# Output blocks of six groups: ScalarE copies and accumulating DMAs in place of VectorE sums, in a new order

## The chip, the core and the metric

The kernel runs on one core of a Trainium2 chip. Time is device time in microseconds (us) from launch to end; three runs of the kernel before are shown, and one further execution was profiled. TensorE multiplies matrices, VectorE and ScalarE work on elements, GpSimd and SyncE (SP) here only issue transfers, and 16 DMA engines move the data.

## The reference

For each of 8 batches an attention goes both ways between 512 tokens and 32 states of 8 heads, and a two-layer net follows on the 544 rows of each batch (4352 x 512 in all):

```python
a = softmax(scale * x @ state.T);   xread = a @ state        # [8, 8, 512, 64]
a2 = softmax(scale * state @ x.T);  sread = a2 @ x           # [8, 8, 32, 64]
r = concatenate([xread, sread], axis=2)                      # -> rows [8 * 544, 512]
h = r @ w_in                                                 # 512 -> 2048
g = where(h >= 1, h, where(h <= -1, 0, (h + 1) ** 2 / 4))
out = g @ w_out                                              # 2048 -> 512
```

## The kernel before

**Arithmetic.** Everything is float32, made of pairs of rounded float32 numbers: an operand is split into a high part (a ScalarE cast) and a low part (a VectorE subtraction), and each product is three matmuls, high by high, low by high and high by low. `xread @ w_in` is computed as `a @ (state @ w_in)`; the weight products `state @ w_in` of a batch are made in pieces (`sw_pair`), whose two parts are named sw_..h and sw_..l. The hidden rows of a batch come in eight units of 256 columns (`Hidden`: the matmuls at L718 to L720, then Relu and Square on ScalarE and a min/max, "bound", on VectorE at L744).

**The second layer.** Batch 0 multiplies by w_out directly (L779 to L781). The other seven are computed as blocks of 2 by 2 with seven products in place of eight: a group g takes a pair of batches and one half of the 2048 columns, so that the pairs (1, 2), (3, 4) and (5, 6) are groups 0 to 5; groups 6 and 7 ("wide", tiles of 384 columns) are batch 7 with the state rows of all batches. Each product k of 1 to 7 has four quarters (steps Qg.k.n, `quarter`, matmuls at L1329). Its operand is a block of hidden values or a difference of blocks, split again by ScalarE (L1292) and VectorE (L1266, `operand_ops`). Its weights are a block of w_out, or a sum of such blocks, of 1 MB, loaded from DRAM into one of eleven shared buffers (L1305, `weight_ops`; r and f are two names for such a buffer).

**Weight sums.** The blocks of w_out go to DRAM once they are split (L1234). For the sums, SP loads one half of a chunk (L1204), GpSimd adds the other half onto it by an accumulating DMA (also L1204), VectorE makes four sums (L1213 to L1216), ScalarE and VectorE split them (L1219, L1223), and SP stores the result (L1201, `block_ops`). There are eight chunks, D0 to D7; products 5, 6, 7 and 3 of a group need the sums of its four chunks.

**Outputs.** The products of a group run in three accumulators in PSUM. After each of the seven (`done_ops`) the accumulator is taken out: X after product 1, Y after 6, C22 after 7 and C21 after 4, all in one accumulator that goes on; V after 5 and C12 after 3; C11 after 2. The four output blocks of a pair are C11 + X, C12 + Y, C22 + V and C21, each summed over the pair's two groups. Before, they live in four buffers of 4 KB per partition ("one" 22, 23, 25, 26): in the first group of a pair ScalarE copies X, V, Y and C21 (L1368), and VectorE adds every other accumulator (L1366). After the second group SP stores the four blocks (L1382).

**Order.** The first 90 us (batch 0 and the splitting of the weights) stand in a table of their own, `ORDER`. The rest is planned when the program is built: `STEPS` sets the order of TensorE's steps (S weight products, X scores, R state reads, U units, G batch 0, Q quarters, L last units), and `Flow.schedule` places the steps of the other engines one by one where each could start first, by given costs and by `LATE`, the time from a step's end until another engine can use its result. On the chip each engine goes through its queue in that order, and waits for semaphores.

Of the kernel before, what the change touches and what calls it, by code (L numbers as in the profile page):

```python
# [13 lines left out]
ALU = mybir.AluOpType  # L14
# [138 lines left out]
class Flow:  # L153
# [4 lines left out]
    LATE = {"SP": 2.6, "PE": 0.3, "ACT": 0.12, "DVE": 0.12}  # L158
# [19 lines left out]
    def late(self, k):  # L178
        return self.LATE[self.ops[k][0]]

# [138 lines left out]
def state_exchange_moe(  # L319
# [17 lines left out]
    nc = tc.nc  # L337
# [695 lines left out]
    with guard:  # L1033
# [7 lines left out]
            r2_0={0: 0.0}, r2_1={0: 0.0}, xt={0: 0.0}, xn={0: 0.0}, z={0: 0.0}, e2={0: 0.0},  # L1041
        )
        flow.kinds.update({kd: (kd, len(flow.rooms[kd])) for kd in ("wc", "att", "tmp", "xt", "xn", "z", "e2", "r2_0", "r2_1")})
# [5 lines left out]
        flow.hold("spare", "spare", 8)  # L1049
        flow.rooms["pair"][10] = plan.done["g2", 1, 0, 6]  # L1050
# [17 lines left out]
        def load_ops(kind, b):  # L1068
            if kind == "xt":
                op(("dma", "xt", b), "SP", 2.6, lambda: load("xt", load_xt, b), take=[("xt", ("xt", b))])  # L1070
            else:
                op(("dma", "xn", b), "SP", 2.6, lambda: load("xn", load_xn, b), take=[("xn", ("xn", b))])
# [37 lines left out]
        def away_ops(b):  # L1110
            op(("away", b), "SP", 1.4, lambda: atts[b].trade_out(), [("exp2", b, 0), ("exp2", b, 1)],
               ends=[] if b == 1 else [("e2", b)])

        def read_ops(b):
            def m(name):
                return lambda: getattr(atts[b], name)()

            load_ops("xn", b)
            op(("trade", b), "SP", 1.4, m("trade_in"), [("away", b)], take=[("tmp", ("e2x", b))])
# [73 lines left out]
        def block_ops(c):  # L1193
# [31 lines left out]
            op(("wa", c), "SP", 1.4, lambda: whole(0), [("dA", c)], take=[("s", ("s", c))])  # L1225
            op(("wb", c), "SP", 1.4, lambda: whole(1), [("wa", c)])
# [3 lines left out]
            op(("dS", c), "SP", 2.6, lambda: store_block(1, place()), [("wsl", c)], ends=[("s", c)])  # L1230

        def keep_ops(c):
# [3 lines left out]
            op(("dA", c), "SP", 2.6, store, [("wol", c)] + ([] if c == NJ - 1 else [("g2", 1, 0, c)]), ends=[("wo", c)])  # L1236
# [4 lines left out]
        C_AT = {"X": 22, "V": 23, "Y": 25, "Z": 26}  # L1241
# [58 lines left out]
        def weight_ops(g, k):  # L1300
# [9 lines left out]
            op(h, "SP", 2.6, fetch_block, [("dA" if BLOCK[k] < 4 else "dS", 4 * (g % 2) + c) for c in range(4)],  # L1310
# [31 lines left out]

        def done_ops(g, k):
            odd = g % 2
            b0 = 1 + g // 2 * 2
            names = {1: ("X", "X"), 5: ("V", "V"), 6: ("Y", "Y"), 3: ("C12", "Y"), 7: ("C22", "V"), 2: ("C11", "X"), 4: ("C21", "Z")}
            name, where = names[k]
            c = ones[C_AT[where]].rearrange("p (d s) -> p d s", d=2)[:, :, :nn(g)]
            final = name[0] == "C"
            add = odd or name in ("C12", "C22", "C11")  # L1350
            need = [("q", g, k, 3)] + ([("away", 1)] if name == "Y" and not g else [])
            if final and k != 4:
                need.append(({"C12": "Y", "C22": "V", "C11": "X"}[name], g))
            if add and odd and not (final and k != 4):
                need.append(({"X": "C11", "V": "C22", "Y": "C12", "C21": "C21"}[name], g - 1))
            if not odd and not add and g:
                need.append(("go", {"X": "C11", "V": "C22", "Y": "C12", "C21": "C21"}[name], g - 1))
            ends = {3: [("B", g)], 2: [("C", g)], 4: [("A", g)]}.get(k, [])

            cut = [slice(d, d + 1) for d in range(2)] if g == 7 and final else [slice(0, 2)]  # L1360

            def evacuate():
                for d in cut:
                    src = chain(g, k)[:, d, :nn(g)]
                    if add:
                        nc.vector.tensor_tensor(out=c[:, d], in0=c[:, d], in1=src, op=ALU.add)  # L1366
                    else:
                        nc.scalar.copy(out=c[:, d], in_=src)  # L1368

            op((name, g), "DVE" if add else "ACT", nn(g) / 448 if add else nn(g) / 526, evacuate, need, ends=ends)  # L1370
            if final and odd:
                i, side = int(name[1]) - 1, int(name[2]) - 1

                def away():
                    if wide(g):
                        o = out[(B - 1) * S:].rearrange("r c -> (r c)")
                        o = o.rearrange("(i d p s t) -> i s p d t", i=2, d=2, p=P, s=2)[i, side]
                    else:
                        r0 = (b0 + side) * S + i * 2 * P
                        o = out[r0:r0 + 2 * P].rearrange("(d p) t -> p d t", p=P)  # L1380
                    for d in cut:
                        (nc.scalar if len(cut) == 2 and d.start else nc.sync).dma_start(out=o[:, d], in_=c[:, d])  # L1382

                op(("go", name, g), "SP", 1.4, away, [(name, g)])


        def sread_ops():
# [25 lines left out]
            op(("away", B), "SP", 1.4, away, [("scale2", b) for b in range(B)])  # L1413
            op(("trade", B), "SP", 1.4, back, [("away", B)], take=[("tmp", "sx")])
# [134 lines left out]
```

## Time and profile before

| | |
|---|---|
| runs shown, us | 616.03 median (615.67, 616.03, 618.26) |
| profiled execution, us | 619.75, of it the span from the first to the last instruction 618.0 |
| TensorE (PE) busy | 595.7 us (96%) |
| VectorE (DVE) busy | 521.4 us (84%) |
| ScalarE (ACT) busy | 402.3 us (65%) |
| GpSimd (POOL) busy | 7.8 us (1%) |
| moved by DMA | 136.97 MB |

Busy shares are of the span. Matmuls overlap: a row's duration is longer than the distance to the next start, and the distance is what a stream of matmuls costs. Queues of SP are shown as SPq; a DMA's landing time is from its issue to its last byte. Waits are attributed to what ended last before the waiting instruction began.

### The profile page before, as it was taken

Reading aid. Unit: us, or ns where it says so; the run is one execution under the profiler, and the core shown is the slowest. Engines: PE = TensorE matmul, PEld = TensorE weight load, DVE = VectorE, ACT = ScalarE, POOL = GpSimd, SP = SyncE. Lnnn points to the kernel's source line nnn. Section 1 sums busy time; section 2 is a strip of 40 time slices with the busy share of each in tenths; the row PEclk is TensorE's granted clock in tenths of the full one; section 3 lists DMA queues with packets and bytes.
Section 4 is the critical chain, followed back from the end, with each engine's and each line's share of the span. In section 5 each row is a group of like instructions: output and inputs, shape, how many; then the busy total and the mean of one; then the engine's idle time right before and its main releaser. Section 6 shows DMA issues by size and latency. Waiting matters only on the chain.

```text
span 618.0 us, 10299 instructions
## 1 busy us (share of the span) xinstructions
PE 595.7 (96%) x4208; PEld 481.3 (78%) x4208; DVE 521.4 (84%) x597; ACT 402.3 (65%) x512; POOL 7.8 (1%) x15
## 2 busy tenths in 40 slices
PE   5999988999999999999999999999999999999997
PEld 2677766677668877878777887788787888989996
DVE  6999977989799999799897987995769848785794
ACT  6999946966686556667656555765665456566741
POOL 0000100010100000000000000000000000000000
PEclk9999997999999999999999999999999999999999
DMA  8999999499976358655676148554727294434284
GB/s 357 425 370 374 362 351 353 153 262 308 291 231 218 98 159 303 187 205 171 203 275 197 43 142 284 167 193 137 230 78 272 86 313 158 139 125 137 79 281 151
DMA packets 81326, 136.97 MB, mean 222 GB/s; under 512 B 3200, under 2 KB 67328, under 8 KB 76160
## 3 DMA queue, kind: packets, MB, share of 16 engines
q1 hardware_dynamic: 79408, 131.28, 61.7%
q0 software_dynamic: 1152, 4.19, 3.7%
q10 hardware_dynamic: 720, 0.85, 0.4%
q8 instruction: 33, 0.54, 0.3%
q14 instruction: 13, 0.11, 0.1%
HBM read 105.91 MB, written 30.41 MB: 221 GB/s over the span
## 4 chain that ended last, share of the span: by engine, by line
PE 73%; DMA 12%; DVE 11%; issue 1%; ACT 1%; POOL 0%; POOLq 0%; DVEq 0%
PE bank L1329 39%; PE bank L718 8%; PE bank L720 8%; PE bank L719 8%; DMA f<-blocks 7%; PE bank L656 3%; DMA r<-blocks 3%; DVE r L1266 2%; DMA blocks<-f 2%; PE bank L779 1%; PE bank L620 1%; PE bank L780 1%; PE bank L781 1%; DVE one L1366 1%; DVE f L1223 1%
## 5 line engine op out<-in xcount | busy, mean ns | idle before, releaser
L1329 PE MATMUL bank<-r,r 128*128 128x512 f32 (+1 forms) x1344 | 301.1, 378 | 4.1 <-DVE r L1266 2.8
L1329 PEld LDWEIGHTS bank<-r,r 128*128 128x128 f32 x1344 | 245.7, 188 | 54.2 <-issue 8.9
L1292 ACT CAST r<-f 128x1024 fp32r<-128x1024 f32 (+1 forms) x140 | 113.1, 835 | 67.7 <-PE bank L1329 36.0
L1266 DVE TENSOR_TENSOR r<-f,r 128x1024 fp32r<-128x1024 f32 (+1 forms) x140 | 129.1, 950 | 10.6 <-ACT r L1292 10.4
L736 ACT ACTIVATE f<-bank,half 128x512 f32<-128x512 f32 x112 | 76.0, 687 | 63.9 <-PE bank L720 62.9
L744 DVE SCALAR_TENSOR_TENSOR f<-f,bank 128x1024 f32<-128x1024 f32 x56 | 67.7, 1211 | 26.8 <-ACT f L740 26.8
L740 ACT ACTIVATE f<-f 128x1024 f32<-128x1024 f32 x56 | 59.3, 1061 | 1.4
L1366 DVE TENSOR_TENSOR one<-one,bank 128x1024 f32<-128x1024 f32 (+2 forms) x44 | 46.3, 1058 | 9.7 <-PE bank L1329 8.1
L1266 DVE TENSOR_TENSOR f<-f,f 128x1024 f32<-128x1024 f32 x36 | 43.5, 1214 | 0.1
L656 PE MATMUL bank<-w,sb 64*32 64x256 f32 x1024 | 33.2, 381 | 2.9 <-DVE w L828 2.1
L1266 DVE TENSOR_TENSOR f<-f 128x384 f32<-128x384 f32 (+1 forms) x44 | 30.8, 732 | 0.1
L656 PEld LDWEIGHTS bank<-w,sb 64*32 64x32 f32 x1024 | 17.1, 106 | 14.0 <-issue 3.9
L779 PE MATMUL bank<-r,r 128*128 128x512 f32 x64 | 25.5, 399 | 0.0
L780 PE MATMUL bank<-r,r 128*128 128x512 f32 x64 | 24.9, 389 | 0.0
L781 PE MATMUL bank<-r,r 128*128 128x512 f32 x64 | 24.9, 389 | 0.0
L1368 ACT COPY one<-bank 128x1024 f32<-128x1024 f32 (+1 forms) x16 | 15.3, 958 | 13.0 <-PE bank L1329 10.7
L718 PE MATMUL bank<-ath,sw_0h 128*128 128x512 f32 (+1 forms) x56 | 21.3, 381 | 1.2 <-DVE one L744 0.8
L720 PE MATMUL bank<-atl,sw_0h 128*128 128x512 f32 (+1 forms) x56 | 21.0, 376 | 0.3 <-DVE atl L557 0.3
L719 PE MATMUL bank<-ath,sw_0l 128*128 128x512 f32 (+1 forms) x56 | 20.9, 374 | 0.0
L718 PE MATMUL bank<-ath,sw_2h 128*128 128x512 f32 x52 | 20.2, 389 | 0.0
L719 PE MATMUL bank<-ath,sw_2l 128*128 128x512 f32 x52 | 20.2, 389 | 0.0
L720 PE MATMUL bank<-atl,sw_2h 128*128 128x512 f32 x52 | 20.2, 389 | 0.0
(198 smaller groups left out, 898.6 us busy)
## 6 DMA issues: line engine op xcount, KB each, us to landing
r<-blocks SPq DMA_DIRECT2D x56, 1024.0 KB, 6.5
xt<-in_xt_dram SPq DMA_DIRECT2D x16, 512.0 KB, 7.4
f<-in_moe_w_in_dram SPq DMA_DIRECT2D x8, 1024.0 KB, 8.9
f<-in_moe_w_out_dram SPq DMA_DIRECT2D x8, 1024.0 KB, 11.2
blocks<-r SPq DMA_DIRECT2D x8, 1024.0 KB, 13.9
xn<-in_x_dram SPq DMA_DIRECT2D x8, 1024.0 KB, 6.3
blocks<-f SPq DMA_DIRECT2D x8, 1024.0 KB, 5.8
out_dram<-one SPq DMA_DIRECT2D x12, 512.0 KB, 7.2
```

Source lines behind the costliest of these rows:

```text
L656: nc.tensor.matmul(banks[hh][pr * NS:(pr + 1) * NS, cols], lhsT=sb[rows, b, pr], rhs=w32[c][rows, pr], start=True, stop=True,)
L718: nc.tensor.matmul(o, lhsT=wh[:, k, sl], rhs=ah[:, k, t], start=first, stop=False)
L719: nc.tensor.matmul(o, lhsT=wl[:, k, sl], rhs=ah[:, k, t], start=False, stop=False)
L720: nc.tensor.matmul(o, lhsT=wh[:, k, sl], rhs=al[:, k, t], start=False, stop=last)
L736: nc.scalar.activation(out=u, in_=h, func=AF.Relu, scale=0.5, bias=half)
L740: nc.scalar.activation(out=u, in_=u, func=AF.Square)
L744: nc.vector.scalar_tensor_tensor(out=u, in0=u, scalar=1.0, in1=h, op0=ALU.min, op1=ALU.max)
L779: nc.tensor.matmul(a, lhsT=lh, rhs=oh, start=f == 0, stop=False)
L1266: nc.vector.tensor_tensor(out=x, in0=y, in1=z, op=ALU.subtract)
L1292: nc.scalar.copy(out=o, in_=v)
L1329: nc.tensor.matmul(o, lhsT=lhs, rhs=v[:, e, a], start=fresh and n == m == 0, stop=n == 3 and m == 2, skip_group_check=not fresh,)
L1366: nc.vector.tensor_tensor(out=c[:, d], in0=c[:, d], in1=src, op=ALU.add)
```

## The change

In groups 0 to 5 ScalarE copies every accumulator (42 copies, 7 a group) into one of four rooms, "one" 22, 23, 25 and 26, which are now handed out by the planner. Each copy goes at once to its block in the output in DRAM: the first of a block by a plain store of SP, the others by a DMA of GpSimd that adds to what is there and waits until the block's transfer before has landed. A room is free again when its transfer has landed. Groups 6 and 7 keep the form of before (`last_ops`). The planner's times change: results of SP's transfers count as usable later (`LATE`, `MORE`), and `STEPS` is a new order of the same steps. Of that table two lines stand here.

```diff
 STEPS = (
-    "S1.1.1.2 X2 G0.7.0 U1.0 G0.7.1 U1.1 S2.0.2.1 U1.2 S1.3.1.4 U2.0 U1.3 U2.1 Q0.1.0 Q0.1.1 Q0.2.0 "
+    "S1.1.1.2 X2 G0.7.0 U1.0 U1.1 G0.7.1 S1.3.1.4 U1.2 S2.0.2.1 U1.3 Q0.2.0 U1.4 U2.0 Q0.1.0 Q0.2.1 "
...
-    LATE = {"SP": 2.6, "PE": 0.3, "ACT": 0.12, "DVE": 0.12}
+    LATE = {"SP": 3.6, "PE": 0.3, "ACT": 0.12, "DVE": 0.12}
+    MORE = {"wa": 2.4, "wb": 3.8, "dA": 5.0, "dS": 2.0, "away": 2.6, "trade": 1.4, "go": 1.5}
...
     def late(self, k):
-        return self.LATE[self.ops[k][0]]
+        return self.LATE[self.ops[k][0]] + self.MORE.get(k[0], 0.0)
...
+        NAMES = {1: "X", 5: "V", 6: "Y", 3: "C12", 7: "C22", 2: "C11", 4: "C21"}
+        BEFORE = {"C11": "X", "C12": "Y", "C22": "V"}
+        FINAL = {v: k for k, v in BEFORE.items()}
...
         def done_ops(g, k):
-            odd = g % 2
-            b0 = 1 + g // 2 * 2
...
-            add = odd or name in ("C12", "C22", "C11")
...
+            name = NAMES[k]
+            need = [("q", g, k, 3)]
             ends = {3: [("B", g)], 2: [("C", g)], 4: [("A", g)]}.get(k, [])
...
+            own = ("c", name, g)
+            block = FINAL.get(name, name)
+
+            def copy():
+                nc.scalar.copy(out=held(own, g), in_=chain(g, k))
+
+            def away():
+                if prior:
+                    nc.gpsimd.dma_start(out=out_of(g, name), in_=held(own, g), accum_op=ALU.add)
+                else:
+                    nc.sync.dma_start(out=out_of(g, name), in_=held(own, g))
+
+            prior = sent.get((g // 2, block))
+            sent[g // 2, block] = ("go", name, g)
+            op((name, g), "ACT", 0.97, copy, need, take=[("c", own)], ends=ends)
+            op(("go", name, g), "SP", 2.0 if prior else 1.45, away, [(name, g)] + [prior] * bool(prior), ends=[own])
...
             def evacuate():
                 for d in cut:
                     src = chain(g, k)[:, d, :nn(g)]
                     if add:
-                        nc.vector.tensor_tensor(out=c[:, d], in0=c[:, d], in1=src, op=ALU.add)
+                        nc.vector.tensor_tensor(out=c()[:, d], in0=c()[:, d], in1=src, op=ALU.add)
```

**VectorE's queue where the second layer begins.** f5 and f4 hold the first two weight chunks of the sums, nm2 and z2 belong to scores, sw1_1l is the low half of the weight product that TensorE's step U1.0 needs. Before:

```order
L1213 TENSOR_TENSOR f4_75<-f4_75 128x256
L1214 TENSOR_TENSOR f4_75<-f4_75 128x256
L1215 TENSOR_TENSOR f4_75<-f4_75 128x256
L1216 TENSOR_TENSOR f4_75<-f4_75 128x256
L1223 TENSOR_TENSOR f5_76<-f5_76 128x1024
L577 TENSOR_REDUCE nm2_0_801<-one24_96 128x1
L578 TENSOR_SCALAR nm2_0_801<-nm2_0_801 128x1
L501 STREAM_TRANSPOSE z2_805<-bank_69 128x1024
L672 TENSOR_TENSOR sw1_1l_760<-bank_69,sw1_1h_759 128x1024
L513 TENSOR_REDUCE m1_2_806<-z2_805 128x32
```

The same place now, where f9 is the second chunk:

```order
L1218 TENSOR_TENSOR f5_76<-f5_76 128x256
L578 TENSOR_REDUCE nm2_0_753<-one24_96 128x1
L579 TENSOR_SCALAR nm2_0_753<-nm2_0_753 128x1
L578 TENSOR_REDUCE nm2_0_753<-one24_96 128x1
L579 TENSOR_SCALAR nm2_0_753<-nm2_0_753 128x1
L1225 TENSOR_TENSOR f5_76<-f5_76 128x1024
L502 STREAM_TRANSPOSE z2_803<-bank_69 128x1024
L673 TENSOR_TENSOR sw1_1l_759<-bank_69,sw1_1h_758 128x1024
L514 TENSOR_REDUCE m1_2_804<-z2_803 128x32
L1215 TENSOR_TENSOR f9_80<-f9_80 128x256
L1216 TENSOR_TENSOR f9_80<-f9_80 128x256
```

The second chunk's sums moved from ahead of sw1_1l to behind it, and a second pair for nm2 moved ahead.

**An output of a second group.** On VectorE before, an accumulator (bank) is added to one22 among the bounds and splits of group 1's operands:

```order
L1266 TENSOR_TENSOR r8_90<-f10_81,r8_90 128x1024
L744 SCALAR_TENSOR_TENSOR f5_76<-f5_76,bank_69 128x1024 x2
L1366 TENSOR_TENSOR one22_94<-one22_94,bank_69 128x1024
L1266 TENSOR_TENSOR f5_76<-f5_76,f7_78 128x2x512
L1266 TENSOR_TENSOR r10_92<-f5_76,r10_92 128x1024
```

On ScalarE now, in group 1, two such accumulators are copied among its casts:

```order
L1293 CAST r0_82<-f10_81 128x1024
L1293 CAST r8_90<-f9_80 128x1024
L1370 COPY one26_98<-bank_69 128x1024
L737 ACTIVATE f7_78<-bank_69,half_104 128x512
L555 CAST ath4_1920<-zt4_1903 128x1024
L737 ACTIVATE f7_78<-bank_69,half_104 128x512
L741 ACTIVATE f7_78<-f7_78 128x1024
L1293 CAST r3_85<-f6_77 128x1024
L1293 CAST r2_84<-f9_80 128x1024
L1370 COPY one23_95<-bank_69 128x1024
```

The work went from VectorE's queue to ScalarE's, and the copy needs no earlier value of its buffer.

**GpSimd's queue.** Before, it ends with the eighth accumulation of weight chunks. Now outputs (out_0_dram) follow, 30 in all, the first of them between two chunks:

```order
L1206 DMA f2_73<-blocks_70 128x1024
L1374 DMA out_0_dram<-one23_95 128x2x512
L1206 DMA f7_78<-blocks_70 128x1024
L1206 DMA f2_73<-blocks_70 128x1024
L1374 DMA out_0_dram<-one22_94 128x2x512
L1374 DMA out_0_dram<-one23_95 128x2x512
L1374 DMA out_0_dram<-one25_97 128x2x512
```

The last two chunks' accumulations stand behind an output's.

## Rows read from the trace of the kernel before

**Rows 1.** The page's head and its busy times by engine.
```profile
span 618.0 us, 10299 instructions
...
PE 595.7 (96%) x4208; PEld 481.3 (78%) x4208; DVE 521.4 (84%) x597; ACT 402.3 (65%) x512; POOL 7.8 (1%) x15
```

**Rows 2.** Stretches: busy us (x instructions) by engine, granted clock, DMA share, GB/s.
```profile
30.00:90.00 60.00, 60.00 (x394) 45.62 (x392) 54.99 (x58) 49.06 (x51) 1.88 (x2) 1.00 1.00 363
90.00:110.00 20.00, 15.45 (x97) 11.59 (x104) 16.45 (x21) 13.49 (x20) 1.72 (x2) 0.83 1.02 364
110.00:180.00 70.00, 65.99 (x438) 48.35 (x418) 63.83 (x72) 53.33 (x69) 3.45 (x4) 1.00 0.81 242
180.00:500.00 320.00, 318.83 (x2419) 255.50 (x2419) 278.89 (x277) 195.49 (x233) 0.00 (x0) 1.00 0.57 186
...
590.00:618.00 28.00, 23.43 (x134) 22.82 (x132) 19.31 (x38) 7.28 (x15) 0.00 (x0) 1.00 0.63 205
```

**Rows 3.** Waits of TensorE: total us, times, longest.
```profile
PE bank L718 <- DVE sw_1l L672: 4.6, 1, 4.6
PE bank L1329 <- DVE r L1266: 2.8, 4, 1.2
...
PE bank L1329 <- DMA r<-blocks: 1.2, 2, 0.8
PE bank L718 <- DVE one L744: 0.8, 1, 0.8
PE bank L718 <- DVE one L1366: 0.8, 1, 0.8
```

**Rows 4.** TensorE in time: start, us, instruction, idle time before it.
```profile
89.73 0.39 PE L781 MATMUL bank<-r,r 128*128 128x512 f32 x1
94.67 0.80 PE L718 MATMUL bank<-ath,sw_7h 128*128 128x512 f32 x1 [4.55 <-DVE sw_1l L672]
...
99.96 0.52 PE L779 MATMUL bank<-r,r 128*128 128x512 f32 x1
100.31 0.39 PE L780 MATMUL bank<-r,r 128*128 128x512 f32 x1
```

**Rows 5.** VectorE in time, the same columns.
```profile
82.11 1.23 DVE L756 TENSOR_TENSOR r<-one,r 128x1024 fp32r<-128x1024 f32 x1
84.01 0.42 DVE L1213 TENSOR_TENSOR f<-f 128x256 f32<-128x256 f32 x1 [0.67 <-DMA f<-blocks]
...
88.88 0.42 DVE L1213 TENSOR_TENSOR f<-f 128x256 f32<-128x256 f32 x1 [3.31 <-DMA f<-blocks]
...
90.35 1.22 DVE L1223 TENSOR_TENSOR f<-f 128x1024 fp32r<-128x1024 f32 x1
...
92.27 1.24 DVE L501 STREAM_TRANSPOSE z<-bank 128x1024 f32<-128x1024 f32 x1
93.43 1.19 DVE L672 TENSOR_TENSOR sw_1l<-bank,sw_1h 128x1024 fp32r<-128x1024 f32 x1
```

**Rows 6.** The second accumulation: GpSimd in time; the chain of waits.
```profile
73.10 0.87 POOL L1204 DMA_DIRECT2D f<-blocks  x1 [0.18 <-issue]
...
73.10 15.75 DMA f<-blocks
```

**Rows 7.** The chain of waits: a run of matmuls without a pause.
```profile
363.53 9.52 PE bank L1329 x42
```

**Rows 8.** Groups of one form: busy us, mean ns, idle before.
```profile
L1366 DVE TENSOR_TENSOR one<-one,bank 128x1024 f32<-128x1024 f32 x30 | 36.3, 1214 | 1.1 <-PE bank L1329 0.7
...
L1368 ACT COPY one<-bank 128x1024 f32<-128x1024 f32 x12 | 12.1, 1010 | 10.1 <-PE bank L1329 7.8 <-PE bank L720 2.3
```

**Rows 9.** GpSimd's DMA queue; its issues; weight loads of 180 to 500 us.
```profile
q0 software_dynamic: 1152, 4.19, 3.7%
...
L1204 POOL DMA_DIRECT2D f<-blocks x8 | 7.1, 882 | 161.6 <-DVE z L536 70.6 <-DVE nm L578 24.9 <-DVE f L1266 24.8
...
DMA to landing us min/median/max: 5.4/6.1/11.4
```

More of the change, by code (lines that the diff above doesn't have):

```diff
@@ L1049, in state_exchange_moe @@
         flow.hold("spare", "spare", 8)
+        flow.hold("c", ("e2", 1), 25)
         flow.rooms["pair"][10] = plan.done["g2", 1, 0, 6]
@@ L1110, in away_ops @@
         def away_ops(b):
[L1111 to L1112 removed]
+            op(("away", b), "SP", 1.45, lambda: atts[b].trade_out(), [("exp2", b, 0), ("exp2", b, 1)],
+               ends=[("e2", b)])
         def read_ops(b):
@@ L1223, in sum_low @@
                 nc.vector.tensor_tensor(out=s.bitcast(F32R), in0=s, in1=place()[:, :1024], op=ALU.subtract)
-            op(("wa", c), "SP", 1.4, lambda: whole(0), [("dA", c)], take=[("s", ("s", c))])
-            op(("wb", c), "SP", 1.4, lambda: whole(1), [("wa", c)])
+            op(("wa", c), "SP", 1.45, lambda: whole(0), [("dA", c)], take=[("s", ("s", c))])
+            op(("wb", c), "SP", 1.45, lambda: whole(1), [("wa", c)])
             op(("ws", c), "DVE", 1.4, sums, [("wb", c)])
@@ L1229, in block_ops @@
             op(("wsl", c), "DVE", 1.14, sum_low, [("wsh", c)])
-            op(("dS", c), "SP", 2.6, lambda: store_block(1, place()), [("wsl", c)], ends=[("s", c)])
+            op(("dS", c), "SP", 2.75, lambda: store_block(1, place()), [("wsl", c)], ends=[("s", c)])
         def keep_ops(c):
@@ L1234, in store @@
                 nc.sync.dma_start(out=blocks[c // 4, 0, :, c % 4], in_=rounded(wo_at[c]).bitcast(F32))
-            op(("dA", c), "SP", 2.6, store, [("wol", c)] + ([] if c == NJ - 1 else [("g2", 1, 0, c)]), ends=[("wo", c)])
+            op(("dA", c), "SP", 2.75, store, [("wol", c)] + ([] if c == NJ - 1 else [("g2", 1, 0, c)]), ends=[("wo", c)])
         BLOCK = {1: 0, 2: 2, 3: 7, 4: 3, 5: 4, 6: 5, 7: 6}
@@ L1308, in fetch_block @@
                 )
-            op(h, "SP", 2.6, fetch_block, [("dA" if BLOCK[k] < 4 else "dS", 4 * (g % 2) + c) for c in range(4)],
+            op(h, "SP", 2.75, fetch_block, [("dA" if BLOCK[k] < 4 else "dS", 4 * (g % 2) + c) for c in range(4)],
                take=[("wt", h)])
@@ new lines, in state_exchange_moe, with out_of @@
+        BEFORE = {"C11": "X", "C12": "Y", "C22": "V"}
+        FINAL = {v: k for k, v in BEFORE.items()}
+        sent = {}
+        def out_of(g, name):
+            i, side = (int(v) - 1 for v in FINAL.get(name, name)[1:])
+            if wide(g):
+                o = out[(B - 1) * S:].rearrange("r c -> (r c)")
+                return o.rearrange("(i d p s t) -> i s p d t", i=2, d=2, p=P, s=2)[i, side]
+            r0 = (1 + g // 2 * 2 + side) * S + i * 2 * P
+            return out[r0:r0 + 2 * P].rearrange("(d p) t -> p d t", p=P)
@@ new lines, in held @@
+        def held(h, g):
+            return ones[flow.place[h]].rearrange("p (d s) -> p d s", d=2)[:, :, :nn(g)]
+        def done_ops(g, k):
+            name = NAMES[k]
+            need = [("q", g, k, 3)]
+            ends = {3: [("B", g)], 2: [("C", g)], 4: [("A", g)]}.get(k, [])
+            if wide(g):
+                return last_ops(g, k, need + [(b, g) for a, b in BEFORE.items() if a == name], ends)
+            own = ("c", name, g)
[11 more added lines that the diff above has]
+            op(("go", name, g), "SP", 2.0 if prior else 1.45, away, [(name, g)] + [prior] * bool(prior), ends=[own])
@@ L1362, in evacuate, with last_ops @@
+        def last_ops(g, k, need, ends):
+            odd, name = g % 2, NAMES[k]
+            block = FINAL.get(name, name)
+            own = ("c", block, B)
+            final = odd and name not in FINAL
+            c = lambda: held(own, g)
+            add = odd or name in BEFORE
+            if odd and name not in BEFORE:
+                need.append((block, g - 1))
+            cut = [slice(d, d + 1) for d in range(2)] if final else [slice(0, 2)]
             def evacuate():
@@ L1365, in evacuate @@
                     if add:
-                        nc.vector.tensor_tensor(out=c[:, d], in0=c[:, d], in1=src, op=ALU.add)
+                        nc.vector.tensor_tensor(out=c()[:, d], in0=c()[:, d], in1=src, op=ALU.add)
                     else:
[L1368 to L1372, printed above, removed]
+                        nc.scalar.copy(out=c()[:, d], in_=src)
+            op((name, g), "DVE" if add else "ACT", nn(g) / 448 if add else nn(g) / 526, evacuate, need,
+               take=[] if add else [("c", own)], ends=ends)
+            if final:
                 def away():
[L1375 to L1380, printed above, removed]
                     for d in cut:
-                        (nc.scalar if len(cut) == 2 and d.start else nc.sync).dma_start(out=o[:, d], in_=c[:, d])
-                op(("go", name, g), "SP", 1.4, away, [(name, g)])
+                        (nc.scalar if d.start else nc.sync).dma_start(out=out_of(g, name)[:, d], in_=c()[:, d])
+                op(("go", name, g), "SP", 1.45, away, [(name, g)], ends=[own])
         def sread_ops():
@@ L1411, in low @@
                 nc.vector.tensor_tensor(out=sl, in0=src, in1=sh.bitcast(F32), op=ALU.subtract)
-            op(("away", B), "SP", 1.4, away, [("scale2", b) for b in range(B)])
-            op(("trade", B), "SP", 1.4, back, [("away", B)], take=[("tmp", "sx")])
+            op(("away", B), "SP", 1.45, away, [("scale2", b) for b in range(B)])
+            op(("trade", B), "SP", 1.45, back, [("away", B)], take=[("tmp", "sx")])
             op(("kept", B), "DVE", 1.2, turn, [("trade", B)], ends=["sx"])
```

23 lines of the change are left out of this document (5 added, 18 removed), and 46 rows, old and new, of the table STEPS.

## The prediction

> **What bounds the kernel now.** I read the busy shares first: TensorE works through 595.7 of 618.0 us [rows 1], so a change can win at most what TensorE idles, plus what it loses to a low clock; a saving on another engine is worth nothing by itself. Next the stretches [rows 2], to see where those 22.3 us lie. From 90 to 110 us TensorE is busy for 15.45 of 20 us at a mean granted clock of 0.83. From 110 to 180 us it idles 4.01 us while VectorE is busy for 63.83 of 70. From 180 to 500 us it idles only 1.17 us, with VectorE at 87%, ScalarE at 61% and the DMA engines at 0.57. From 590 us on it idles 4.57 us, of which 1.2 is one wait [rows 3] and the rest the store behind the last matmul. What these leave of the 22.3, some 8 us, lies in the first 30 us, before the code that the change touches. Then the waits by name [rows 3]: the largest that the change can reach is 4.6 us, once, for the low half of a weight product (sw_1l); all others together are some 6 us in pieces of at most 1.2.
>
> That one wait is the place to look at closely. TensorE ends a matmul at about 90.1 us and starts the next at 94.67 [rows 4]. VectorE explains it [rows 5]: its queue is in order, and the four sums of the second weight chunk stood ahead of sw_1l. They waited 3.31 us for a transfer; then came the sums, their low half, a maximum, a transpose, and only then sw_1l. The transfer is an accumulating DMA of GpSimd, issued at 73.10 and 15.75 us in landing [rows 6]. And the idle time costs twice. Behind it matmuls start 0.43 us apart, at the lower of the two clock levels (1.2 GHz), until 99.96; the thirteen starts from 94.67 to 100.31 took 5.64 us [rows 4]. At the full clock a matmul of 512 columns takes 9.52/42 = 0.227 us [rows 7], thirteen 2.95. So the stall cost 4.55 + 2.69 = 7.2 us. The 4.01 us of short waits between 110 and 180 us left the mean clock there at 1.00 [rows 2].
>
> **Removed, added, moved.** *Output adds.* Thirty VectorE adds of 1.21 us go (36.3 us busy), and ScalarE copies of 1.01 us rise from 12 to 42, or 30.3 us more [rows 8]. Of this I count nothing: from 180 us on, where nearly all of it lies, TensorE has work in 99.6% of the time, and ScalarE goes from 61% to about 70% of that stretch. The cover is gone only where an engine queue runs late. The copy is shorter than the add that it replaces, so the matmuls that wait for a freed accumulator do not wait longer.
>
> *Transfers.* Twelve output stores of before become twelve plain stores and 30 accumulating ones. The trace has no accumulation into DRAM; nearest are GpSimd's eight accumulations from DRAM into SBUF, of the same 512 KB. Their queue took 3.7% of 16 engines' span [rows 9], 22.9 us for eight, so 2.9 us of all engines each. Bounds: a plain 512 KB transfer at half of this, and twice it for a read beside the write, so 1.4 to 5.8; I take 2.9, as the nearest row adds as well. Thirty make 86 us, which lifts the DMA share from 180 to 500 us from 0.57 to about 0.8. Who could wait? First the weight loads of TensorE (1 MB; 35 of them in that stretch landed in 5.4 to 11.4 us, median 6.1 [rows 9]). I counted in both orders the matmuls between the one that frees a load's room and the first that reads the load, at 0.227 us. In the order of before the room for a load is as short as 6.1 us and is under 10 us ten times; in the new order the shortest are 8.7 and 8.8 and the others 10.9 or more. A load that meets a whole accumulation lands after 6.1 + 2.9 = 9.0 us, which fits all but two. Second, ScalarE, whose copy waits until the transfer out of its room has landed, with all casts behind it. In the new order each of the four rooms is refilled no sooner than after 23.8 us of matmuls, and the longest landing of this kind of transfer was 15.75 us [rows 6]. So I take 1.2 us of TensorE idle time here, as before; the bounds are 0 and 6.
>
> The Trainium skill ("DMA: Bandwidth & Descriptors", section "Issuing engines are not separate DMA queues") says that transfers from SP, ScalarE and GpSimd run on the same 16 engines and interleave, whoever issues them; that speaks against the change. The trace agrees: the accumulation issued at 73.10, beside the loads and stores of 70 to 90 us, took 15.75 us [rows 6]. What this would make of the time is the third rival below.
>
> *New order at the stall.* In the new order VectorE's queue, from the same point (83.2 us, the end of the row at 82.11 [rows 5]), holds the sums of the first chunk alone, two maxima, their low half, the transpose, and sw_1l; the second chunk's sums stand behind it. By the durations of the same rows: sums from 84.01, if the first transfer lands as before, to 85.48; two maxima of 0.79 (90.35 to 92.27, less 1.13 for the low half) to 87.06; low half 88.2; transpose 1.16 to 89.35; sw_1l 1.19 to 90.5. TensorE reaches it at 90.1 as now, so 0.4 us of stall is left of 4.55, and a wait that short left the clock alone elsewhere. Gain: 4.15 + 2.69 = 6.8 us.
>
> *The stretch behind it.* TensorE now arrives some 7 us earlier, but VectorE does not work faster. I followed both queues to the third quarter of product 2 (Q0.2.2). VectorE has 33.3 us of work from 84.0 to that operand's low half (three chunks' sums at 1.47, sixteen operations and three low halves at 1.13, three transposes at 1.16, three maxima and some small ones): 117.3. TensorE has 102 matmuls at 0.227 and two weight products at 1.0 from 90.5: 115.7. So it stalls there for 1.6 us. The load for product 6 is issued when product 1 is done, and only 6.0 us of matmuls lie between; beside other transfers I expect 7.5 us, so 1.5 us (bounds 0 and 5). One more microsecond for what I did not follow makes 4.1 us, against the 4.01 of before. Gain here: 0; bounds 4 us better, 5 worse.
>
> *The end.* The last two groups keep their adds on VectorE and the last 27 us their kind of order; I leave its wait of 1.2 us as it is (bounds 0 and 2.5).
>
> **Sum.** 6.8 us less; of the profiled execution's own 619.75 us (span 618.0 and 1.75 around it) this makes 612.9. That execution is 3.7 us above the median of the runs shown, 616.03, and I carry the difference over: **609.2 us**. One measurement of this kernel tells about 0.5%, 3.1 us, from no change.
>
> **Rivals.** *More than the one stall goes.* The new order was drawn with longer transfer times, so other waits on late chunks may go too. If all of the idle time after 90 us goes (10.9 us, of it 4.55 the stall) with the 2.7 of the clock, 13.6 us are won: 602.4; half of the rest gives 605.8. For it speaks that every wait from 110 to 180 us is for VectorE [rows 3]; against it the 33.3 us of VectorE work just counted.
>
> *The stall moves.* VectorE was busy 63.83 of 70 us behind the stall [rows 2] and caught up while TensorE stood still. If 5 of the 6.8 us come back as waits for its operands before 180 us, the time is 614.2. Against it: its own idle time in the stretch, 3.31 us at one place [rows 5], goes as well.
>
> *Slower: accumulations delay the weight loads.* Place: matmuls of the first six groups, 180 to 500 us. If loads landed in 12 us instead of 6.1, the thirteen with under 12 us of matmuls in the new order would wait 14.0 us in sum: 616.0 - 6.8 + 14 = 623.2. It decides from about 11.3 us of landing, where the waits eat the 6.8. For it: the longest loads took 11.4. Against it: the median, and a DMA share of 0.8 on average.
>
> *GpSimd issues late.* The Trainium skill ("SBUF — State Buffer", the box on the trap in which VectorE blocks a GpSimd DMA) warns that GpSimd cannot write descriptors while VectorE holds their shared port. The eight issues of before took 0.88 us each [rows 9], all in stretches in which VectorE was busy over 80% of the time [rows 2], so the trace shows none of it. As a mechanism of this kernel: transfers issued late hold their rooms longer, and the copies, casts and matmuls wait. It takes over 8 us of delay on top of the longest landing before the first room is late; with ten copies held 1 us each it gives 619.
>
> **How the numbers follow.** Forecast 0.62, with its own range 605 to 613 (the first stall sure within 1 us, the stretch behind it from 4 better to 5 worse, the middle up to 5 worse); more goes 0.15; the stall moves 0.12; slower loads 0.08; late issues 0.03. Faster by over 0.5% (below 612.9): 0.60 + 0.15 = 0.75. Slower (above 619.1): the loads and part of the late issues, 0.09. Within: 0.16. The range 603.5 to 616.5 leaves out the best third of the first rival and all of the slow ones.
>
> **What would show it.** Right: no TensorE idle time over 1 us near 90 us, granted clock 1.00 from 90 to 110, VectorE's sw_1l ahead of the second chunk's sums; a wait of 1 to 3 us near 117; VectorE some 35 us less busy, ScalarE 30 more, both without effect; 180 to 500 us (now some 7 us earlier) still with TensorE over 99% busy. Wrong: weight loads with a median over 10 us and TensorE waits for them of several microseconds; ScalarE copies that wait for an output transfer; or a TensorE stall over 3 us elsewhere before 180 us with the clock down behind it.

## The result and the profile after

The changed kernel takes **623.17 us** (median of 18 executions, 616.25 to 627.11); the kernel before, on the same chip, took 615.73 (613.56 to 619.51). The ratio is 1.0092, 95% interval 1.0064 to 1.0119: **slower by 0.9%**, where 609.2 us and a gain were forecast. Ratios, here and below, compare executions in the faster state and are not quotients of the medians, which would give 1.012 here. The profiled execution is the longest of the 18, 627.11 us; run 12 below shows a shorter one.

The page, with GpSimd's DMA queue [rows 1, 9]:

```profile
span 625.3 us, 10392 instructions
...
PE 598.9 (96%) x4208; PEld 482.3 (77%) x4208; DVE 489.1 (78%) x567; ACT 429.0 (69%) x542; POOL 43.8 (7%) x45
...
q0 software_dynamic: 9312, 19.93, 19.0%
```

The waits of TensorE [rows 3]:

```profile
PE bank L1330 <- DMA r<-blocks: 14.8, 5, 6.5
...
PE bank L1330 <- DVE sw_0l L673: 0.8, 1, 0.8
...
PE bank L1330 <- ACT r L1293: 0.6, 1, 0.6
```

The span is 7.3 us longer. TensorE idles 26.4 us instead of 22.3, and is busy 3.2 us longer with the same 4208 matmuls; 2.0 of that is time at the low clock (4.7 us, worked out below, against 2.7). The weight product's 4.6 us wait is gone from the list; 14.8 us for weight loads stand at its head, where 1.2 stood. VectorE is 32 us less busy and ScalarE 27 us more, and neither ends a long wait. The stretches [rows 2], in the same columns, and three short ones around two waits:

```profile
90.00:110.00 20.00, 19.22 (x138) 14.31 (x137) 19.55 (x23) 17.69 (x23) 1.72 (x2) 1.00 1.04 357
110.00:180.00 70.00, 63.91 (x433) 47.82 (x431) 58.69 (x68) 49.86 (x66) 5.94 (x6) 0.98 0.90 272
180.00:500.00 320.00, 310.17 (x2334) 246.72 (x2335) 244.32 (x244) 211.28 (x250) 28.66 (x24) 0.98 0.82 223
...
147.00:153.00 6.00, 5.99 (x78) 4.59 (x79) 2.40 (x3) 0.66 (x3) 0.00 (x0) 0.72 0.28 89
170.00:186.00 16.00, 9.45 (x55) 6.97 (x53) 13.23 (x14) 9.94 (x12) 3.01 (x3) 0.87 1.05 287
186.00:192.00 6.00, 6.00 (x70) 3.26 (x70) 0.14 (x1) 1.01 (x1) 0.00 (x0) 0.50 0.22 62
```

From 90 to 110 us the loss is gone: 3.77 us more of TensorE's work, at a clock of 1.00 instead of 0.83. VectorE in time shows how [rows 5]:

```profile
87.40 1.24 DVE L502 STREAM_TRANSPOSE z<-bank 128x1024 f32<-128x1024 f32 x1
88.57 1.18 DVE L673 TENSOR_TENSOR sw_1l<-bank,sw_1h 128x1024 fp32r<-128x1024 f32 x1
...
90.80 0.41 DVE L1215 TENSOR_TENSOR f<-f 128x256 f32<-128x256 f32 x1
```

The low half stands ahead of the second chunk's sums and is done at 89.75, just before TensorE begins U1.0 at 89.84; and those sums no longer wait either (no idle time stands on the row). U1.0 does not read this low half: its operands are sw_7h and sw_7l [rows 4], pieces of a weight product made earlier. By the kernel, what it waited for before is a pair of PSUM banks to write into, free once the low half, the last operation to read them, is done. In run 13 below U1.0 runs ahead of that low half.

What was lost lies behind. TensorE in time, at the first quarters of products 6 (Q0.6) and 4 (Q0.4) of group 0:

```profile
147.01 2.31 PE L1330 MATMUL bank<-r,r 128*128 128x512 f32 x6 [4.30 <-DMA r<-blocks]
...
185.89 2.93 PE L1330 MATMUL bank<-r,r 128*128 128x512 f32 x6 [6.55 <-DMA r<-blocks]
188.75 3.57 PE L657 MATMUL bank<-w,sb 64*32 64x256 f32 x64
```

Both wait for their weights. The chain of waits gives the loads' issue and time to landing, 10.82 and 15.47 us:

```profile
136.05 10.82 DMA r<-blocks
...
170.38 15.47 DMA r<-blocks
```

After each the clock is down: 0.72 from 147 to 153 us and 0.50 from 186 to 192, so 6.0 x 0.28 + 6.0 x 0.50 = 4.7 us more. The two waits cost 10.85 + 4.7 = 15.5 us, twice what the 90 us stall cost. Behind 190 us there are three more, of 0.25, 1.94 and 1.75 us. All but the wait at Q0.4 are known at this size from this one execution only. The DMA engines while the load for product 4 (Q0.4) is under way, 170 to 186 us (queues; issues with KB and median us to landing):

```profile
q1 hardware_dynamic: 1870, 3.00, 53.4%
q0 software_dynamic: 560, 1.57, 51.6%
...
f<-blocks POOLq DMA_DIRECT2D x2, 512.0 KB, 9.9
r<-blocks SPq DMA_DIRECT2D x1, 1024.0 KB, 15.5
e_there<-one SPq DMA_DIRECT2D x1, 512.0 KB, 16.1
out_dram<-one POOLq DMA_DIRECT2D x1, 512.0 KB, 13.6
e_x<-e_there SPq DMA_DIRECT2D x4, 128.0 KB, 14.8
```

Nine transfers, the load among them, the first six issued within two us: the 16 engines are full until it lands (share 1.05). One of the nine is an accumulation into the output; two are accumulations for the weight sums of group 1, issued at 170.16 and 171.37; in the kernel before these two came at 156.71 and 169.12. By the Trainium skill ("DMA: Bandwidth & Descriptors", section "Issuing engines are not separate DMA queues") transfers run on the same 16 engines and interleave, whichever engine starts them; the trace agrees: SP's queue (q1) and GpSimd's (q0) share the engines, and their shares sum to the full.

The copies and the accumulations as groups [rows 8]:

```profile
L1370 ACT COPY one<-bank 128x1024 f32<-128x1024 f32 x42 | 42.5, 1013 | 34.5 <-PE bank L1330 34.3
L1374 POOL DMA_DIRECT2D out_dram<-one x30 | 36.2, 1208 | 335.5 <-ACT one L1370 319.9 <-issue 8.1 <-DMA out_dram<-one 7.5
```

Landing of the accumulations, of the weight loads of 110 to 180 us, and of those of 180 to 500 us [rows 9]:

```profile
DMA to landing us min/median/max: 5.4/9.1/13.6
...
DMA to landing us min/median/max: 7.4/10.0/15.5
...
DMA to landing us min/median/max: 5.4/8.3/13.9
```

q0's 19.0% of 625.3 us is 118.8; the eight accumulations of the weight sums keep 22.2 (first run below), so 96.6 for 30, **3.2 us of all 16 engines each**, where 2.9 was forecast. ScalarE's copies wait for TensorE alone, never for a transfer out of their room.

### The profile page after: what moved, and what is told of

Read it like the earlier page. It is cut to its first block, busy times and chain, and to the rows that moved or that the text cites. A ratio compares the mean times of both kernels' runs of the same rounds, so it can differ in the third digit from the quotient of the medians.

```text
span 625.3 us, 10392 instructions
## 1 busy us (share of the span) xinstructions
PE 598.9 (96%) x4208; PEld 482.3 (77%) x4208; DVE 489.1 (78%) x567; ACT 429.0 (69%) x542; POOL 43.8 (7%) x45
## 3 DMA queue, kind: packets, MB, share of 16 engines
q0 software_dynamic: 9312, 19.93, 19.0%
## 4 chain that ended last, share of the span: by engine, by line
PE 84%; DMA 12%; DVE 2%; ACT 1%; issue 1%; SPq 0%; ACTq 0%
PE bank L1330 42%; DMA r<-blocks 10%; PE bank L719 9%; PE bank L721 9%; PE bank L720 9%; PE bank L657 5%; PE bank L780 2%; PE bank L781 2%; PE bank L782 2%; DMA out_dram<-f 1%; PE bank L621 1%; PE bank L485 1%; DMA sb<-in_state_dram 1%; ACT f L737 0%; ACT r L1293 0%
## 5 line engine op out<-in xcount | busy, mean ns | idle before, releaser
L1330 PE MATMUL bank<-r,r 128*128 128x512 f32 (+1 forms) x1344 | 302.2, 380 | 16.7 <-DMA r<-blocks 14.8
L1370 ACT COPY one<-bank 128x1024 f32<-128x1024 f32 x42 | 42.5, 1013 | 34.5 <-PE bank L1330 34.3
L1374 POOL DMA_DIRECT2D out_dram<-one x30 | 36.2, 1208 | 335.5 <-ACT one L1370 319.9
L657 PE MATMUL bank<-w,sb 64*32 64x256 f32 x1024 | 35.0, 395 | 0.5 <-DVE w L829 0.5
```

Source lines behind the costliest of these rows:

```text
L657: nc.tensor.matmul(banks[hh][pr * NS:(pr + 1) * NS, cols], lhsT=sb[rows, b, pr], rhs=w32[c][rows, pr], start=True, stop=True,)
L1330: nc.tensor.matmul(o, lhsT=lhs, rhs=v[:, e, a], start=fresh and n == m == 0, stop=n == 3 and m == 2, skip_group_check=not fresh,)
L1370: nc.scalar.copy(out=held(own, g), in_=chain(g, k))
```

## Experiments

Theory A: the accumulations delay the weight loads. Theory B: the new order bunches transfers, so that loads come late even without them. The "30 left out" below are the accumulating output transfers; those accumulators then never reach the output. Medians are in us, ratios against the kernel before on the same chip.

| run | median | ratio, 95% interval |
|---|---|---|
| changed kernel | 623.17 | 1.0092 (1.0064 to 1.0119) |
| 1 the 30 left out | 614.37 | 0.9978 (0.9955 to 1.0001) |
| 2 the 30 as plain stores | 617.96 | 1.0025 (1.0000 to 1.0049) |
| 3 old steps, new outputs | 655.99 | 1.0639 (1.0597 to 1.0681) |
| 4 new steps and times, old outputs | 638.15 | 1.0373 (1.0329 to 1.0416) |
| 5 Q0.4 later | 614.14 | 0.9956 (0.9922 to 0.9990) |
| 6 Q0.4 and Q0.6 later | 624.34 | 1.0112 (1.0086 to 1.0138) |
| 7 group 0's three left out | 617.07 | 1.0012 (0.9983 to 1.0042) |
| 8 both later, the 30 left out | 623.20 | 1.0088 (1.0059 to 1.0117) |
| 9 Q0.4 later, the 30 left out | 610.49 | 0.9897 (0.9870 to 0.9925) |
| 10 Q0.4 later, Q0.6 by a quarter | 649.75 | 1.0547 (1.0500 to 1.0594) |
| 11 X3 later | 634.07 | one execution |
| 12 changed kernel again | 625.34 | 1.0154 (1.0088 to 1.0220) |
| 13 old steps and outputs, new times | 630.47 | 1.0206 (1.0164 to 1.0249) |
| 14 new steps and outputs, old times | 630.52 | 1.0214 (1.0167 to 1.0261) |

**1 and 2. The transfers.**

```diff
-                    nc.gpsimd.dma_start(out=out_of(g, name), in_=held(own, g), accum_op=ALU.add)
+                    return                                                   # run 1
+                    nc.gpsimd.dma_start(out=out_of(g, name), in_=held(own, g))   # run 2
```

> The changed kernel without its 30 accumulating output transfers (so 30 of the 42 copied accumulators never reach the output); every other instruction stands where it stood. Theory A, the accumulations delay the weight loads: the loads' median landing goes back from 8.0 to about 6.1 to 6.5 us, the waits of 4.3 us (Q0.6) and 6.6 us (Q0.4) shrink to under 2 us each, the TensorE clock behind them stays at 1.00, and the time is 605 to 611 us. Theory B, the new order bunches the loads itself (at 170 us a weight load, a trade, two chunk accumulations stand within 2 us, and only one output transfer): at least 8 of the 10.9 us at these two places stay, and the time is 614 to 620 us.

> The changed kernel with the 30 accumulating transfers turned into plain stores to the same place from the same queue (the sums are left out, the last accumulator written stands in the output). Every instruction stands where it stood. If what hurts is the work that an accumulation is for the DMA engines (about 3.2 us of all 16 each, by the queue's 118.8 us less some 23 for the eight chunk accumulations), half of it goes: loads land in about 7 us and the time is 612 to 618 us, between the run without the transfers and the changed kernel. If what hurts is the queue or the moment of issue and not the volume, the time stays at 619 to 625 us. If only the new order hurts, it is within 3 us of the run without the transfers.

Run 1, the waits of TensorE:

```profile
PE bank L1330 <- DMA r<-blocks: 6.6, 3, 5.5
```

The load for Q0.4 in its chain of waits:

```profile
167.14 14.41 DMA r<-blocks
```

And its stretch from 180 us:

```profile
180.00:500.00 320.00, 318.41 (x2381) 255.37 (x2382) 245.80 (x247) 217.18 (x257) 0.00 (x0) 0.99 0.56 184
```

Their q0, of run 1:

```profile
q0 software_dynamic: 1152, 4.19, 3.6%
```

and of run 2:

```profile
q0 software_dynamic: 5472, 19.93, 9.9%
```

Both theories hold a part. Without the transfers the wait at Q0.6 is gone (its load lands in 6.67 us instead of 10.82; run 12 shows that it can be gone with them too), loads from 180 to 500 us land in 6.0 us (median) and make no wait there apart from Q0.4's, and 1.1% is won back, less than theory A claimed. But Q0.4 still waits 5.49 us, for a load that takes 14.41: that wait belongs to the order. A plain store costs (61.0 - 22.2) / 30 = 1.3 us of all engines, an accumulation 2.5 times as much, and run 2 lies between run 1 and the changed kernel: what hurts is the engines' work, and not GpSimd's queue alone, which has the same 30 transfers in run 2.

**3 and 4. The order and the outputs apart.** Run 3 is the changed kernel with the `STEPS` of before, run 4 the kernel before with the new `STEPS`, `LATE` and `MORE`.

> The changed kernel's outputs (42 copies, 12 plain stores, 30 accumulating transfers) with the order of steps of the kernel before. Theory A: the 90 us stall of 4.6 us with its low clock is back, and room for a weight load is as short as 6.1 us and under 10 us ten times in this order, so waits for loads sum to 15 us or more from 110 us on: 625 to 640 us. Theory B: the loads of the old order are not bunched, the stall is back, and the time is that of the kernel before, 613 to 620 us.

> The kernel before, outputs summed on VectorE, with the new order of steps and the new late times of the planner. Theory A: the gain of 6.8 us at 90 us stays and little is given back, 605 to 611 us, with Q0.6 and Q0.4 waiting under 2 us each. Theory B: long waits for the weight loads of Q0.6 and Q0.4 (4 us and more) stand here too, 614 to 620 us. A third way, VectorE's 30 adds that stand between its other work in an order drawn without them: waits of TensorE for VectorE's operands of 5 us and more from 110 to 180 us, 614 to 622 us.

TensorE's waits in run 3, and in run 4:

```profile
PE bank L1330 <- DMA r<-blocks: 29.2, 10, 7.3
```

```profile
PE bank L719 <- DVE sw_2l L673: 5.1, 1, 5.1
...
PE bank L657 <- DVE f L745: 3.7, 1, 3.7
PE bank L657 <- DVE sw_6l L673: 3.3, 1, 3.3
```

Run 3 is worse than theory A asked: in the old order, with its short room, ten waits for loads sum to 29.2 us. It has the new times as well, which in the old order cost 2.1% by themselves (run 13), so its 6.4% is not the outputs' alone. Run 4 went the third way, though 16 us beyond its window: with the adds back on VectorE the new order waits for VectorE, and no wait of TensorE for a load is over 1 us. Each half of the change alone is far worse than both, as if the order had been drawn for the outputs. One expectation failed in run 3: the 90 us stall did not come back. Runs 13 and 14 go after that.

**5, 6 and 10. More room for a load.** Run 5 moves two quarters of product 4 of group 0 (6 also two of product 6, 10 those by one quarter only):

```diff
-    Q0.3.1 Q0.4.0 S2.6.2.7 S3.0.3.1 Q0.4.1 Q0.3.2 Q0.3.3 Q0.4.2
+    Q0.3.1 S2.6.2.7 S3.0.3.1 Q0.3.2 Q0.3.3 Q0.4.0 Q0.4.1 Q0.4.2    # 5, 6, 10
-    Q0.5.1 Q0.6.0 R0 Q0.6.1 Q0.5.2 Q0.5.3 U1.5 Q0.6.2
+    Q0.5.1 Q0.5.2 Q0.5.3 U1.5 Q0.6.0 R0 Q0.6.1 Q0.6.2              # 6
+    Q0.5.1 Q0.5.2 Q0.6.0 R0 Q0.6.1 Q0.5.3 U1.5 Q0.6.2              # 10
```

> The changed kernel with one place of its order altered: the first two quarters of group 0's product 4 stand behind the two chunk steps and the last two quarters of product 3, which puts about 6.3 us of matmuls (3.57 for the chunk steps, 2.7 for the two quarters) between the issue of the load for Q0.4 and its first use. If the place in the order makes this wait, it goes from 6.55 us to under 1.5, its low clock goes too, and the time is 613 to 618 us. If the load lands as late as the engines have work beside it (the trade, the accumulations and the chunks of the next group follow it), the wait only moves: 619 us or more.

> The same, and product 6 of group 0 begins behind the last two quarters of product 5 and a hidden unit step, 5.4 us of matmuls later after the issue of its load. If room between issue and use is all that both long waits lack, the 4.3 us wait at Q0.6 goes as well and the time is 608 to 613 us: under the kernel before, with all 30 accumulations in it. If the accumulations hurt in sum, by the many short waits from 180 us on and not at these two places, the time stays above 614 us.

> The order with product 4 later, and product 6 of group 0 behind one more quarter of product 5 (1.4 us of matmuls more room for its load), all 30 accumulations in it. If only the room counts, the executions with a wait at Q0.6 lose it and the time falls by 1 to 3 us, to 611 to 613. If, as in the run with both places altered, the planner's other moves (the chunk loads now stand ahead of product 6) make VectorE's operands late, waits of 5 us and more for VectorE and ScalarE come in and the time is 618 to 625 us.

Run 5, the load for Q0.4 in the chain:

```profile
163.42 16.27 DMA r<-blocks
```

TensorE where it reads it:

```profile
179.73 4.40 PE L1330 MATMUL bank<-r,r 128*128 128x512 f32 x18 [1.52 <-DMA r<-blocks]
```

And two stretches:

```profile
110.00:180.00 70.00, 67.19 (x510) 50.23 (x509) 65.47 (x79) 55.48 (x72) 5.92 (x6) 1.00 0.98 298
180.00:500.00 320.00, 318.48 (x2331) 255.82 (x2331) 245.68 (x240) 216.49 (x256) 31.08 (x26) 1.00 0.85 230
```

The load takes as long as before (16.27 us); TensorE has other work meanwhile, waits 1.52 us, and the clock stays at 1.00. (This profile is of one of its shortest executions, 610.95 us of 610.45 to 620.34; it has no wait at Q0.6 either, whose place is as before.) The time is 1.4% under the changed kernel and 0.4% under the kernel before, with all 30 accumulations in it and a DMA share of 0.85: **the fastest version with the whole output**. Run 6 also ends every wait for a load (0.2 us is left), but not the waiting:

```profile
PE bank L1330 <- ACT r L1293: 3.4, 4, 0.9
PE bank L657 <- DVE sw_6l L673: 2.9, 1, 2.9
PE bank L719 <- DVE sw_7l L673: 2.7, 1, 2.7
```

Here the planner placed chunk loads and VectorE's operations elsewhere as well, operands come late, and the time is that of the changed kernel. Run 10 came out in neither window and went wrong altogether: VectorE idles 12.29 us for a chunk's transfer, ScalarE's in-order queue 17.38 us for that chunk's sums, and behind it stands the cast that TensorE needs (VectorE and ScalarE in time):

```profile
164.68 0.42 DVE L1215 TENSOR_TENSOR f<-f 128x256 f32<-128x256 f32 x1 [12.29 <-DMA f<-blocks]
...
166.31 1.04 ACT L1221 CAST f<-f 128x1024 fp32r<-128x1024 f32 x1 [17.38 <-DVE f L1218]
```

TensorE's longest wait there:

```profile
PE bank L1330 <- ACT r L1293: 27.1, 3, 26.0
```

**7, 8 and 9. Which transfers, and the two causes together.** Run 7 issues the accumulations only `if g`, so without group 0's three; runs 8 and 9 are runs 6 and 5 with the 30 left out.

> The changed kernel without the three accumulating output transfers of group 0 (those accumulators never reach the output), the other 27 as they are. The transfer issued at 138.1 us lies beside the load for Q0.6, issued at 136.1: if that one transfer makes the 4.3 us wait, the wait falls under 0.5 us (0.14 us was seen without all 30), Q0.4 still waits 5 to 7 us, and the time is 616 to 620 us. If the volume from 180 us on is what costs, it stays at 621 us or more.

> Both places of the order altered and the 30 accumulating transfers left out (those accumulators never reach the output): what the new order could give without any price of the transfers. If the two causes add up, no wait over 1.5 us is left after 90 us and the time is 603 to 608 us, the 6.8 us and a little more that were forecast; the difference to the run with both places altered and all transfers is then what the transfers still cost, 3 to 6 us.

> The order with product 4 of group 0 later, and the 30 accumulating transfers left out (those accumulators never reach the output). If the two causes add up, it is the run with that order (614.1) less what the transfers still cost there, or the run without transfers (614.4) less the wait at Q0.4 (5.5 us and the low clock behind it): 605 to 609 us, and that is what the new order is worth without a price of the transfers. If the wait of Q0.4 was all that the transfers fed, it stays at 612 to 615.

In run 7 the wait at Q0.6 falls from 4.30 to 1.59 us, not to under 0.5; Q0.4 still waits, 3.99 us where 5 to 7 were expected. Run 8 missed: the waits for late operands of run 6 are here without any transfer, so they are the planner's. Runs 1, 5 and 9 make a square with the changed kernel. Leaving the transfers out is worth 1.1% in the order as changed and 0.6% with Q0.4 later; moving Q0.4 is worth 1.4% with the transfers and 0.8% without. With Q0.4 later and no transfers the new order wins 1.0%, 6.3 us, between the two windows named for run 9; it is near the 6.8 forecast for the whole change, but of another kernel.

**11. What makes Q0.4's load late.** The scores X3 and with them batch 3's trade through DRAM (e_there, e_x) are moved behind it.

> The changed kernel with batch 3's attention scores (X3) moved from before product 7 of group 0 to behind the first quarter of product 4, so that its trade through DRAM is issued behind the load for Q0.4. If the trade beside the load is what makes it land in 14 to 16 us (it did so without any accumulation too), the load lands in under 10 us here. If it lands in 13 us or more all the same, the two chunk accumulations and the chunk loads do it. The time itself says little, since VectorE's work moves too.

It landed in 12.62 us, in neither window: with the trade gone from beside it, 2.85 us less than on the page, in one execution. So the trade alone is not the cause. That the chunks' and the output's accumulations make the rest is argued and not tested: no run takes the chunks' away, and without the output's the load took 14.41 (run 1).

**12. The changed kernel again.**

> The changed kernel as it is, profiled once more: its executions lie between 616 and 627 us, and the profiled one was the longest of them. If the wait of 6.6 us at Q0.4 belongs to the order, it stands in this execution too (5 to 7.5 us, as in the runs without accumulations and with plain stores), whatever its time. If the wait at Q0.6 hangs on whether the first accumulation meets the load, it may be anything from 0.1 to 4.5 us, and with under 1.5 us there the execution takes 616 to 621 us.

This execution took 618.2 us. TensorE at the two places, from 140 us on:

```profile
139.84 4.45 PE L1330 MATMUL bank<-r,r 128*128 128x512 f32 x18
...
181.20 2.93 PE L1330 MATMUL bank<-r,r 128*128 128x512 f32 x6 [7.46 <-DMA r<-blocks]
```

Q0.4 waits as ever, 7.46 us; Q0.6 does not wait: it is the last six of the eighteen matmuls from 139.84 on, which follow on each other (its load took 6.3 us). So the wait at Q0.4 is of every execution of this order looked at (runs 1, 2, 7 and 12 and the page), that at Q0.6 is not, and a part of the spread from 616 to 628 us is probably of this kind.

**13 and 14. What took the 90 us stall away.** Run 13 is the kernel before with only `LATE` and `MORE` new, run 14 the changed kernel with only those as before.

> The kernel before with the planner's new late times alone: order of steps, adds on VectorE and outputs as before. If these times are what took the stall at 90 us away, it is gone or under 1 us here too and, if nothing else moves for the worse, the time is 607 to 612 us. In this build VectorE's low half of the weight product stands behind the sums of both chunks and two more operations (five places later than before), so the stall may as well stay or grow: then 614 to 622 us, and the times work only together with the new order of steps.

> The changed kernel with the planner's old late times: new order of steps, copies and accumulating transfers. VectorE's rows around the first weight product read as in the kernel before (both chunks' sums ahead of the low half), so if the times and not the order of steps or the missing adds removed the stall, it is back with 3 to 5 us at 90 us and its low clock behind it, and the time is 626 to 635 us. If the stall does not come back, the order of steps removed it, and the time is near 623.

Both missed. In run 14 VectorE's queue stands as before at 90 us, the sums of both chunks ahead of the low half, and the wait is 0.40 us: the second chunk's transfer, issued at 73.56, landed in 9.9 us, not in 15.75 [rows 6]. It is issued 3.6 us behind the first (69.94), not 1.2; in the changed kernel it is 6.1 us (68.53 and 74.65), and 9.0 of landing. Whether the distance is the reason was not tested. The stall came one chunk later, by the same mechanism (VectorE and TensorE in time):

```profile
109.88 0.42 DVE L1215 TENSOR_TENSOR f<-f 128x256 f32<-128x256 f32 x1 [4.92 <-DMA f<-blocks]
...
113.76 2.93 PE L1330 MATMUL bank<-r,r 128*128 128x512 f32 x6 [6.28 <-DVE sw_0l L673]
```

In run 13 the stall at 90 us is two of 1.46 and 0.97 us, for copies of ScalarE that stand behind casts of the chunks' sums. U1.0 begins at 91.54 there, 5.5 us before VectorE's sw_1l, so it does not read it (TensorE and VectorE in time):

```profile
91.54 0.50 PE L719 MATMUL bank<-ath,sw_7h 128*128 128x512 f32 x1 [1.46 <-ACT f L786]
...
96.99 1.22 DVE L673 TENSOR_TENSOR sw_1l<-bank,sw_1h 128x1024 fp32r<-128x1024 f32 x1
```

Waits for VectorE up to 3.1 us come in later. In run 13 the sums of both chunks still stand ahead of sw_1l, so the new times alone do not push them behind it. Of steps, times and outputs, each combination tried that lacks one or two (runs 3, 4, 13 and 14) is slower than all three.

## Why the prediction was wrong

- *The stall at 90 us, 6.8 us.* Right in place and size: nothing over 1 us stands there, the clock is 1.00, and from 90 to 110 us 3.77 us more work and the 2.69 of the clock make 6.5. The reason was half of it: the queue's new order was named, but run 14 shows that the transfer that the sums wait for also takes some 6 us less, by which the stall would have gone in the old order of the queue too. That was luck. And sw_1l was taken for an operand of U1.0, which it is not; as TensorE waits for its end either way, the sum did not suffer.
- *Q0.2.2 at about 117 us, 1.6 us.* About right: 1.1 us, in two pieces of 0.60 and 0.53.
- *Product 6's load, 1.5 us (bounds 0 and 5).* The mechanism was right, the size too small on the page: 4.30 and 1.7 for the clock, with 10.82 us of landing where 7.5 was taken. It varies between executions: there is none in run 12, with the same kernel, and 0.15 us in run 1, without the accumulations.
- ***One more microsecond for what I did not follow.* This step failed.** It held product 4's load: 6.55 us and 3.0 for the clock, and the wait stands in both executions profiled (6.55 and 7.46). Between its issue and TensorE's want of it lie 8.96 us (170.38 to 179.34). The prediction names no wait there, and against the 9.0 us of landing that it took for every load this room would have cost nothing. What it had wrong is the landing: 15.47 us, where 9.0 came from the median of a stretch with a DMA share of 0.57. From 110 to 180 us the median was 10.0, and at Q0.4 nine transfers met. In sum the page has 12.0 us of idle time from 110 to 186 us (6.09 and 5.89) and 4.7 for the clock, where 4.1 was forecast: 12.6 us more, of 14.0 by which the time was missed. It is the last of the signs that the prediction named for being wrong, a stall over 3 us with the clock down behind it.
- *Accumulations, 2.9 us each; middle idle 1.2 us.* 3.2 us, and the share from 180 to 500 us 0.82 for the 0.8 forecast. From 180 us on, without Q0.4's wait, 3.9 us of idle time (310.17 busy, 5.89 of the wait), inside the bound of 6; the low clock, for which nothing was put behind these waits, came with the two long ones alone (4.30 and 6.55 us; at 1.94 and 1.75 it stayed at 1.00).
- *Adds and copies worth nothing; no copy waits for its room.* Right.
- *The slower rival.* Its sign came true, its place did not, and that its 623.2 us came true is luck: it put the loss from 180 to 500 us and at 12 us of landing, where the median is 8.3 and only 3.9 us were lost. Most of the loss lies from 140 to 190 us, and of the 2.0% between run 9 and the changed kernel the place of Q0.4 makes 0.8% even without a transfer. Late issues of GpSimd: its issues took 1.21 us each and no copy, cast or matmul waited for them.

What stays open: the square of runs 1, 5 and 9 leaves about 0.5% that order and transfers cost only together, no more than the four intervals allow (0.6%), so it is not shown; how the loads' delay divides among the transfers of the bunch was not measured one by one; and where the 1.1% of the transfers lies in an execution of usual length is not shown, since the page is of the longest one.

## What to carry to other kernels

A transfer's landing is a matter of its moment: take it from the bunch of transfers issued around it, not from the median of a calm stretch, and set the room of *every* load against it, above all where a new order starts the next phase's loads. A wait of several us costs its length and again 0.4 to 0.6 of that in the clock behind it (1.7, 2.7 and 3.0 us for waits of 4.30, 4.55 and 6.55). When a saving on an idle-covered engine is bought with DMA work, give the loads more room in the same edit: one line of the order (run 5) turned 0.9% lost into 0.4% won; and rebuild with care where a planner decides, since runs 6 and 10 moved the same quarters and two more, and lost.

## Not expected of the hardware

An accumulating DMA of 512 KB into DRAM took 3.2 us of all 16 engines and landed in 9.1 us (median), a plain one from the same queue 1.3 and 6.7; GpSimd's issue took 1.21 us for the one and 0.73 for the other. The packets rise from 144 to 272 each ((5472 - 1152) / 30 and (9312 - 1152) / 30), for the same bytes by the page.
